# An attention, expert and mixer kernel on one core: batch 0's value products in float32, and every stage-1 score by one float32 product

## Chip, core and metric

One core of a Trainium2 chip runs the whole program. The metric is the device time of one execution in microseconds; lower is better. TensorE (PE in the rows, with its weight loads as PEld), VectorE (DVE), ScalarE (ACT), GpSimd (POOL) and the queue engine SyncE (SP) each run their own list of instructions in order and wait for one another through semaphores.

## What is computed

Three stages follow one another, for 4 batches of 576 positions. Stage 1 is attention with 8 heads of 64 and a decay by the cumulated logarithm of f. Stage 2 is attention by 4 experts over the 512 columns that stage 1 gives, mixed by a gate that keeps the best two. Stage 3 is a mixer over positions and a two-layer network of width 2048.

```python
scores = scale * q @ k.T + (cum[:, None] - cum[None, :])     # stage 1, 32 heads, causal
x = softmax(scores) @ v
...
y = sum over e of w[e] * (softmax(scale * (x wq[e]) (x wk[e]).T) @ (x wv[e])) @ wo[e]   # stage 2, 16 heads
...
u = y + (y.T @ U @ V).T                                       # stage 3
out = u + relu(u @ w_ch1) @ w_ch2
```

## The kernel before

**Order.** The kernel is written as many small generators, one for each piece of work. A planner (class `Plan`) resumes them by estimated times, a penalty `PEN` times a priority from the table `PR`, and for some pieces a choice of engine (`Any`, with the handicaps in `BIAS`). What it writes down is a fixed order on each engine. `HEADS` is the order in which score products are made: the 8 heads of batch 0, then `NEXT[b]` heads of the next batch, then the 4 expert heads of batch b, then the rest of the next batch.

**Precision.** Most products must be better than float16. An operand is split into a float16 high part and a float16 rest (`split`, or `parts` for exponentials), and a product is made by three float16 products (`TERMS`).

**Scores.** The first `WHOLE` = 10 heads of stage 1 have one float32 product per block of rows (`YW` tiles, 68 rows of operands: 64 of the head and 4 that carry the decay). The other 22 heads have two rounded-float32 products: one with `X`, which holds high parts and rests, and one with `Y`. For these, `load_heads` issues three loads from GpSimd's queue (`Y`, and `X` twice) and one from SyncE's (`R`), and `lows` makes two subtractions on GpSimd.

**Softmax.** `softmax` (five blocks of rows, 64 to 576 columns) finds the maxima on VectorE and the exponentials on ScalarE into `sc`. From there two ways lead to the value product. A pair of heads within `TURN` is turned on TensorE (`turn_head`): 15 transposes into PSUM, five copies to float16 on ScalarE and five rests on VectorE, both into `pt`. Other pairs are split first (`parts` into the tiles `P`, high part on ScalarE or VectorE, rest on VectorE or GpSimd) and turned by DMA transposes from SyncE's queue. `TURN` holds all of batch 0 (8 heads and 4 experts) and the first pair of batch 1.

**Values.** `values(b)` loads v into `vr` and splits it into `V1`; `values_gates` splits the experts' values into `V2`. `pair_pv` makes the value product of a head, 15 blocks times three terms, 65 columns each (the 65th sums the exponentials), and `pv_out` divides.

**Weights and the filler.** `prep` turns float64 weights into float32 with ScalarE, VectorE and GpSimd; `fold` multiplies wo into w_ch1 (`wfr`); `wf_scaled` and `w2_scaled` split `wfr` and `w2x` in two. `mix(b)` ends with the split of z(b) on ScalarE and VectorE. From then on `hidden` (`hid<-z,wfr`) and `outputs` (`acc<-w2x,g`) have work for batch b. It fills TensorE between the products of later heads.

Of the kernel before, what the change touches and what calls it, by code (L numbers as in the profile page):

```python
# [25 lines left out]
BIAS = {'act': 100.0, 'dve': 1000.0, 'pool': 0.0}  # L26
# [5 lines left out]
XHB = 1  # L32
PBUFS = (1, 1, 1)
VGAT = (2, 2)
EARLY = 11
WHOLE = 10
QUEUE = ('act', 'act', 'sp', 'act')
ACTDMA = 100
PEN = 13.823999999999998
# [5 lines left out]
PR = {'load': 2.75, 'low0': -1.5, 'low': 6.0, 'zeros': -2.0, 'scores': 3.25, 'soft0': 1, 'soft2_0': 1.0, 'soft': 5.5, 'soft2_': 7.0, 'pv0': -1.0, 'pv': 1.75, 'pvout0': 2.0, 'pvout': 4.75, 'project0': 3.75, 'project': 2.25, 'vg0': 0.75, 'vg': 4.75, 'out0': 1.0, 'out': 3.0, 'values0': 1.0, 'values': -1.0, 'wall': 5.25, 'prep': 6.5, 'f64': -1.25, 'f64_2': 3.25, 'fold': 2.25, 'wf': 1.75, 'w2': 3.75, 'mix': 0.25, 'relu': 0.0, 'store': 2.75, 'hidden': 6.25, 'outputs': 8.25}  # L45
TERMS = ((0, 0), (0, 1), (1, 0))

TURN = {(1, 0): 4, (2, 0): 2, (1, 1): 1, (1, 2): 0}

NEXT = (2, 0, 0, 0)  # L50
# [193 lines left out]
def attn_moe_mixer(ctx: ExitStack, tc: tile.TileContext, qk, v, f, wall, wot, wo, w1, w2, u3, v3, out):  # L244
# [161 lines left out]
    V2 = [const.tile([128, KB, 4, 65], F16, name=f"V2{i}") for i in range(2)]  # L406
    V1 = [[const.tile([128, KB, 2, 65], F16, name=f"V1{i}{n}") for n in range(VB[1])] for i in range(2)]
# [16 lines left out]
    r_X, r_Y = ring(XYB[0], "X"), ring(XYB[1], "Y", [68, 2, 576], F32R)  # L424

    YW = [r_Y.make([128, 2, 576], F32, f"YW{i}") for i in range(min(XYB[1], WHOLE))]
    r_Y.first = [YW[(i - WHOLE) % XYB[1]] for i in range(WHOLE)]
    r_R = ring(1, "R", [128, 576], F32)
# [6 lines left out]
    r_vr = ring(VB[0], "vr", [128, KB, 128], F32)  # L435
# [14 lines left out]
    l_v2 = lock("v2")  # L450

# [22 lines left out]
    def load_heads():  # L474
        for i, key in enumerate(HEADS):
            kind, b, h = key
            if i == 2:
                yield ev("rows of first")
            if i < WHOLE:
                Y = yield r_Y  # L480
                HG[key] = (Y,)
                HY[key] = Y
                yield QUEUE[1]
                n = count(2, "loaded", key)
                n.done(dma(HG[key][0][0:64], qk[b, h].rearrange("t d s -> d t s"), queue(1)).t)
                spawn(rows(n, b * H + h, Y), 0)
            elif kind == 1:
                X = yield r_X.of([128, 2, 576], F32R, "X")
                Y = yield r_Y
                HG[key], HY[key] = (X, Y), Y  # L490
                src = qk[b, h].rearrange("t d s -> d t s")
                n = count(4, "loaded", key)
                yield "pool"
                high = [dma(Y[0:64], src, nc.gpsimd)]
                yield "pool"
                high.append(dma(X[64:128], src, nc.gpsimd))
                R = yield r_R
                yield "sp"
                got = dma(R, qk[b, h].rearrange("t d s -> (t d) s"))
                yield "pool"  # L500
                n.done(dma(X[0:64, 1, :], qk[b, h, 1], nc.gpsimd).t)
                spawn(lows(n, X, Y, R, high, got), PR['low0' if b == 0 else 'low'])
                spawn(rows(n, b * H + h, Y), 0)
# [18 lines left out]
    def rows(n, i, Y):  # L522
        yield ev("aug", i // H)
        if id(Y) in map(id, YW):
            yield ev("rows", id(Y))
        yield QUEUE[0]
        a = aug[i]
        n.done(dma((Y if id(Y) in map(id, YW) else Y.bitcast(F32))[64:68], bass.AP(tensor=a.tensor, offset=a.offset, ap=[[S, 4], [2 * S, 2], [1, S]]),
                   queue(0)).t)
        if i == 0:  # L530
            ev("rows of first").done()
# [4 lines left out]
    def lows(n, X, Y, R, high, got):  # L536
        yield got
        for i, H_ in enumerate((Y, X)):
            yield high[i]
            yield "pool"  # L540
            o = slice(64 * i, 64 * i + 64)
            pool("tensor_tensor", X[o, i, :], in0=R[o], in1=H_[o, i, :].bitcast(F32), op=ALU.subtract)
            n.done()
        r_R.free(R)


    def scores():
        yield ev("mask")
        for key in HEADS:
            yield ev("loaded", key)  # L550
            whole, early = key in HEADS[:WHOLE], key in HEADS[:EARLY]

            ops = [(x[:, 0], x.rearrange("d t s -> d (t s)")) for x in HG[key]]
            for blk in range(KB):
# [4 lines left out]
                for c0, c1 in ([(0, n)] if n <= 512 else [(0, 288), (288, 576)]):  # L559
                    w = max(c1 - c0, 256) if key[0] == 1 and not whole else c1 - c0  # L560
# [11 lines left out]
            if key[0] == 1:  # L572
                r_Y.free(HY.pop(key))
# [68 lines left out]
    def turn_head(key):  # L642
# [5 lines left out]
        for c, blks, k0, k1 in ((0, (0, 1), 0, 5), (3, (2,), 0, 5), (6, (3,), 0, 5), (10, (4,), 0, 4), (14, (4,), 4, 5)):  # L648
# [15 lines left out]
            def out_(r=r, bank=bank, flat=flat, c=c, i=i):  # L664
                hi, lo = (pt[:, 15 * t + c:15 * t + c + i, :].rearrange("k c q -> k (c q)") for t in range(2))
# [30 lines left out]
    def pair_pv(kind, b, p):  # L696
# [7 lines left out]
        on_pe = p < TURN.get((kind, b), 0)  # L704
# [4 lines left out]
        for j in range(2):  # L709
# [17 lines left out]
            for blk in range(KB):  # L727
# [11 lines left out]
        if kind == 1:  # L739
            for i in range(2):  # L740
                r_vp[i].free(vs[i])
        elif p == 1:
            l_v2.free(l_v2.held)

    def pv_out(kind, b, p, j, bank, pv):

        h = 2 * p + j
        if kind == 1:
# [5 lines left out]
        if kind == 1:  # L754
            ts(rr, pv[:, :, 64], EPS, ALU.add, RV[b][p // 2], ALU.mult)
        else:
            ts(rr, pv[:, :, 64], EPS, ALU.add)
# [10 lines left out]
        tt(xn, pv[:, :, 0:64], rr[:, :, None].to_broadcast([128, KB, 64]), ALU.mult)  # L768
# [28 lines left out]

    def values(b):

        es, ss, last = [], [], []  # L800
        for half in range(2):
            mx = col(f"mxv{b}{half}", 2)
            vrs = []
            for i in range(2):
                vr = yield r_vr
# [4 lines left out]
                got = dma(vr, v[b][:, :, hp * 128:(hp + 1) * 128], queue(3))  # L810
                vrs.append((vr, got))
            for i, (vr, got) in enumerate(vrs):
                yield got
                junk = yield r_xn.of([128, KB, 128], F16, "junk")
# [6 lines left out]
            if half == 1:  # L821
# [4 lines left out]
                RV[b] = [times(f"rv{b}{i}", s, SV[b][1]) for i, s in enumerate(ss)]  # L826
                ev("sv", b).done()
            for i, (vr, got) in enumerate(vrs):
                hp = 2 * half + i
                hi = yield r_vp[0]  # L830
                lo = yield r_vp[1]
                VP[b, hp] = (hi, lo)
                x = vr.rearrange("p k (h d) -> p k h d", h=2)
                yield from split(hi[:, :, :, 0:64], lo[:, :, :, 0:64], x, ss[half])
                r_vr.free(vr)
# [42 lines left out]
    def values_gates(b):  # L878
# [13 lines left out]
        def out_(tb, nr, pp):  # L892
            x = pp[:nr, :256].rearrange("p (h d) -> p h d", h=4)
            yield from split(V2[0][:nr, tb, :, 0:64], V2[1][:nr, tb, :, 0:64], x, float(2.0 ** -PROJ_EXP))
# [466 lines left out]
    def zero_rows():  # L1361
        for y in YW:
# [6 lines left out]
    def zeros():  # L1369
# [5 lines left out]
        for hl in range(2):  # L1375
# [9 lines left out]
            nc.gpsimd.memset(V2[hl][64:128, 4, :, :], 0.0)  # L1385
            plan.cost += 250
            for t in [V2[hl], *V1[hl]]:
                yield "pool"
                nc.gpsimd.memset(t[:, :, :, 64:65], 1.0 - hl)
                plan.cost += 120  # L1390
# [15 lines left out]
    spawn(zeros(), PR['zeros'])  # L1406
    spawn(scores(), PR['scores'])
# [64 lines left out]
```

## Time and profile before

| | |
|---|---|
| median of 3 runs | 783.21 us (783.13 to 785.93) |
| profiled execution: its time, its span | 780.9 us, 779.2 us |
| TensorE busy, weight loads busy | 672.5 us (86%), 468.7 us (60%) |
| VectorE, ScalarE, GpSimd busy | 488.5 us (63%), 426.4 us (55%), 302.0 us (39%) |
| mean granted TensorE clock | 0.938 |

The four splits of z(b) start at 230.1, 380.9, 535.3 and 666.6 us in the trace. Busy time is the sum of an engine's instructions; TensorE's overlap one another, so its busy time is an upper reading. The span runs from the first instruction to the last, and 1.7 us of the execution lie around it. [...]

### The profile page before, as it was taken

The page shows a single profiled execution, that of the slowest core. Times are in us where ns is not written, and L with a number is a line of the kernel's source. Part 1 is how long each engine was busy: PE and PEld are TensorE (multiplying, and loading weights), DVE is VectorE, ACT ScalarE, POOL GpSimd, SP SyncE. Part 2 cuts the span into 40 slices and gives each one's busy share as a digit, 9 for nine tenths or more (in the row PEclk, how much of TensorE's full clock was granted, in tenths as well). Part 3 has the DMA queues.
Part 4 walks back from the last instruction along what each step waited for, and adds up shares of the span by engine and source line. Part 5 has one row for each costly group of instructions (what it writes and reads, how often), then busy time and mean ns, then how long its engine had stood idle before and what let it go on. Part 6 is the DMA issues. An engine that isn't in the chain of part 4 may idle for free. (4 is left out here: it accounts for less than half of the span.)

```text
span 779.2 us, 15886 instructions
## 1 busy us (share of the span) xinstructions
PE 672.5 (86%) x5810; PEld 468.7 (60%) x5810; DVE 488.5 (63%) x1573; ACT 426.4 (55%) x894; POOL 302.0 (39%) x364
## 2 busy tenths in 40 slices
PE   3777899986476999999699898996999999899996
PEld 2456678665453667666466575664677656555653
DVE  5798876778989854776866367657672763311111
ACT  3676775787686953656666346557562752212121
POOL 4133143236885630477675115666750241000000
PEclk9998999996855999999899999997999999999998
DMA  8534344677995855999997649999973775000000
GB/s 223 145 84 133 77 133 144 173 191 198 165 231 115 166 99 118 150 206 203 235 197 158 128 99 184 190 187 234 188 147 46 165 110 73 28 1 27 1 28 28
DMA packets 203234, 105.40 MB, mean 135 GB/s; under 512 B 164756, under 2 KB 184212, under 8 KB 203124
## 3 DMA queue, kind: packets, MB, share of 16 engines
q1 hardware_dynamic: 182740, 79.37, 51.2%
q0 software_dynamic: 8096, 16.22, 10.7%
q10 hardware_dynamic: 12320, 8.78, 4.1%
q8 instruction: 46, 0.75, 0.4%
q14 instruction: 32, 0.26, 0.1%
HBM read 51.90 MB, written 5.16 MB: 73 GB/s over the span
## 5 line engine op out<-in xcount | busy, mean ns | idle before, releaser
L262 PE MATMUL acc<-w2x,g 128*128 128x512 f16 x768 | 180.2, 380 | 0.5 <-ACT g L267 0.4
L285 POOL TENSOR_TENSOR P<-sc,P 64x64 f16<-64x64 f32 (+4 forms) x127 | 98.2, 779 | 139.4 <-ACT P L267 108.8
L262 PEld LDWEIGHTS <-g 128*128 128x128 f16 x864 | 82.4, 98 | 85.0 <-issue 0.7
L267 ACT ACTIVATE sc<-sc,nm 128x576 f32<-128x576 f32 (+4 forms) x185 | 100.3, 555 | 45.4 <-DVE nm L273 39.1
L262 PE MATMUL hid<-z,wfr 128*128 128x256 f16 x864 | 116.3, 284 | 8.7 <-DVE z L273 3.9
L273 DVE SCALAR_TENSOR_TENSOR g<-hid,g 128x512 f16<-128x512 f32 x72 | 49.6, 689 | 117.6 <-ACT g L267 117.6
L262 PEld LDWEIGHTS <-wfr 128*128 128x128 f16 x864 | 84.5, 101 | 33.7 <-issue 8.8
L267 ACT ACTIVATE g<-hid 128x512 f16<-128x512 f32 x72 | 42.5, 590 | 101.4 <-PE acc L262 72.4
L267 ACT ACTIVATE P<-sc 128x448 f16<-128x448 f32 (+4 forms) x167 | 71.7, 458 | 23.3 <-DMA pt<-P 21.5
L262 PE MATMUL mm<-V,pt 128*128 128x65 f16 x2058 | 75.6, 198 | 4.7 <-DMA pt<-P 3.4
L262 PEld LDWEIGHTS <-pt 128*128 128x128 f16 x2058 | 71.1, 101 | 8.0 <-DMA pt<-P 4.1
L262 PE MATMUL sp<-X 128*128 128x256 f32 (+1 forms) x132 | 53.7, 416 | 23.7 <-DVE nm L273 13.9
L273 DVE TENSOR_TENSOR P<-sc,P 128x576 f16<-128x576 f32 (+4 forms) x43 | 36.4, 847 | 30.8 <-ACT P L267 30.4
L273 DVE CUSTOM_DVE_ANT_0 sc<-sp,mask 128x448 f32<-128x448 f32 (+4 forms) x110 | 46.3, 425 | 9.5 <-POOL P L285 3.9
L285 POOL TENSOR_TENSOR xh<-xn,xh 128x320 f16<-128x320 f32 x29 | 26.3, 908 | 66.9 <-ACT xh L267 56.8
L262 PEld LDWEIGHTS sp<-X 128*128 128x128 f32 x132 | 28.3, 214 | 38.0 <-DVE nm L273 22.2
L262 PE MATMUL mm<-xt,wall 128*128 128x288 f16 x384 | 49.5, 286 | 0.0
L285 POOL TENSOR_TENSOR x<-x,sg 128x512 f32<-128x512 f32 (+2 forms) x18 | 23.1, 1286 | 65.8 <-DVE x L273 52.2
L262 PE MATMUL sp<-Y 68*128 68x256 f32 (+1 forms) x132 | 43.5, 336 | 0.0
L262 PEld LDWEIGHTS <-wall 128*128 128x128 f16 x384 | 37.5, 98 | 9.0
L273 DVE CUSTOM_DVE_ANT_0 sc<-sp,mask,cols 128x320 f32<-128x320 f32 (+4 forms) x75 | 35.8, 486 | 7.2 <-POOL P L285 3.8
L285 POOL TENSOR_TENSOR X<-R,Y 64x576 fp32r<-64x576 f32 x22 | 32.3, 1468 | 15.4 <-DMA R<-in_qk 15.2
(153 smaller groups left out, 1223.5 us busy)
## 6 DMA issues: line engine op xcount, KB each, us to landing
wd<-in_w SPq DMA_DIRECT2D x32, 512.0 KB
Y<-in_qk POOLq DMA_DIRECT2D x22, 288.0 KB, 4.8
R<-in_qk SPq DMA_DIRECT2D x22, 288.0 KB
X<-in_qk POOLq DMA_DIRECT2D x22, 288.0 KB, 6.0
vr<-in_v ACTq DMA_DIRECT2D x16, 320.0 KB
out_dram<-o SPq DMA_DIRECT2D x18, 256.0 KB
Xh<-stg SPq DMA_DIRECT2D x16, 216.0 KB
X<-in_qk POOLq DMA_DIRECT2D x22, 144.0 KB, 4.8
```

The source lines that it names most:

```text
L262: nc.tensor.matmul(out_, lhsT=lhsT, rhs=rhs, start=start, stop=stop, **kw)
L267: nc.scalar.activation(out_, in_, fn, **kw)
L273: getattr(nc.vector, op)(**kw)
L285: getattr(nc.gpsimd, op)(out=out_, **kw)
```

## The change

Scores: the split forms `X`, `R` and `lows` are gone. All 32 heads of stage 1 load one `Y` tile (a ring of three) from ScalarE's queue and have one float32 product per block. Value products of batch 0: `turn_head` copies the turned exponentials once, as float32; v stays in `vr` as loaded, the experts' values go to `V2F` as float32; `pair_pv` makes one float32 product per block where three float16 ones stood. The float16 tiles of values share their space with these float32 tiles and are prepared by `halves_v1` and `halves_v2` when batch 0 is done with them. The pair of batch 1 leaves `TURN`. The planner's tables change as well.

```diff
-BIAS = {'act': 100.0, 'dve': 1000.0, 'pool': 0.0}
+BIAS = {'act': 400.0, 'dve': 1800.0, 'pool': 0.0}
-EARLY = 11
-WHOLE = 10
+EARLY = 14
-TURN = {(1, 0): 4, (2, 0): 2, (1, 1): 1, (1, 2): 0}
+TURN = {(1, 0): 4, (2, 0): 2}
-NEXT = (2, 0, 0, 0)
+NEXT = (2, 0, 4, 0)
...
-            if i < WHOLE:
-                Y = yield r_Y
...
-            elif kind == 1:
-                X = yield r_X.of([128, 2, 576], F32R, "X")
...
-                spawn(lows(n, X, Y, R, high, got), PR['low0' if b == 0 else 'low'])
+            if kind == 1:
+                HY[key] = yield r_Y
+                HG[key] = (HY[key],)
                 yield QUEUE[1]
                 n = count(2, "loaded", key)
+                n.done(dma(HY[key][0:64], qk[b, h].rearrange("t d s -> d t s"), queue(1)).t)
+                spawn(rows(n, b * H + h, HY[key]), 0)
...
+                if as_is(*key[:2]):
+                    to = pt.rearrange("k c q -> k (c q)").bitcast(F32)[:, 128 * c:128 * (c + i)]
+                    if (yield Any(act=110 + 0.833 * 128 * i, dve=110 + 1.04 * 128 * i)) == "act":
+                        copy_scaled(to, flat[:, :128 * i])
+                    else:
+                        dve("tensor_copy", out=to, in_=flat[:, :128 * i])
...
-            for blk in range(KB):
+            for blk in range(KB if whole else 0):
+                yield "pe"
+                for kb in range(blk + 1):
+                    g = 128 * ((0, 1, 3, 6, 10)[blk] + kb)
+                    mm(pv[:, blk, :], pt.rearrange("k c q -> k (c q)").bitcast(F32)[:, g:g + 128],
+                       vs[:, kb, 65 * j:65 * j + 65] if kind == 1 else V2F[:, kb, 2 * p + j, :], blk + kb == 0, kb == blk,
+                       rate=1.7, skip_group_check=True)
+            for blk in range(0 if whole else KB):
...
+    def as_is(kind, b):
+
+        return b == 0 and TURN.get((kind, b), 0) == (4, 2)[kind - 1]
...
+                if as_is(1, b):
+                    VP[b, hp] = vr
+                    ev("vp", b, hp).done()
+                    continue
...
+            if as_is(2, b):
+                yield "act"
+                copy_scaled(V2F[:nr, tb, :, 0:64], x, float(2.0 ** -PROJ_EXP))
```

On TensorE, at the first value products of batch 0 (before; `V_78` and `V_80` are a high part and a rest of v, each product with its own weight load of `pt`):

```order
L658 MATMUL mm<-identr,sc_100 128x128 x4
L262 MATMUL sp<-YW_96 128x320
L262 LDWEIGHTS pt
L262 MATMUL mm<-V_78,pt 128x65
L262 LDWEIGHTS pt
L262 MATMUL mm<-V_78,pt 128x65
L262 LDWEIGHTS pt
L262 MATMUL mm<-V_80,pt 128x65
```

The same place after the change (`vr_79` is v as loaded; a float32 product carries its weight loads in itself):

```order
L632 MATMUL hid<-identr,sc_98 128x128 x3
L261 MATMUL mm<-vr_79,pt 128x65 x10
L261 MATMUL mm<-identr,cols 128x128
L632 MATMUL hid<-identr,sc_99 128x128 x4
L261 MATMUL mm<-vr_79,pt 128x65 x5
L261 MATMUL acc<-Y_94 128x288 x2
```

A head's 45 float16 products became 15 float32 products; they are cut in two only where the planner put transposes between them.

On VectorE, one head of batch 0 before (`ISA sp` and `ISA acc` are the passes that add the mask and find the maxima, `ISA nm` reads them out, `pt` rows are the rests of turned exponentials):

```order
L273 SCALAR_TENSOR_TENSOR pt<-hid,pt 128x512
L273 ISA sp,nm<-sp,mask 128x448
L273 ISA nm 128x1
L273 SCALAR_TENSOR_TENSOR pt<-mm,pt 128x128
L273 SCALAR_TENSOR_TENSOR pt<-mm,pt 128x384
L273 ISA acc,nm<-acc,mask 128x288
L273 ISA nm 128x1
L273 SCALAR_TENSOR_TENSOR pt<-hid,pt 128x384
L273 ISA acc,nm<-acc,mask,nm 128x288
```

And after:

```order
L272 ISA sp,nm<-sp,mask 128x448
L272 ISA nm 128x1
L272 ISA acc,nm<-acc,mask 128x288
L272 ISA nm 128x1
L272 ISA sp,nm<-sp,mask 64x64
L272 ISA nm 64x1
L272 ISA acc,nm<-acc,mask,nm 128x288
```

The rests are gone from VectorE; no copy of turned exponentials stands there in their place, all 60 stand on ScalarE.

On GpSimd, while heads of batch 1 are loaded (before):

```order
L293 DMA Y<-in_qk 64x2x576
L285 TENSOR_TENSOR wfr<-wfr 128x512
L293 DMA X<-in_qk 64x2x576
L285 TENSOR_TENSOR P_75<-sc_100,P_75 128x448
L293 DMA X<-in_qk 64x576
L285 TENSOR_TENSOR P_75<-sc_101,P_75 128x576
L285 TENSOR_TENSOR X<-R,Y 64x576
```

These loads are on ScalarE's queue after the change:

```order
L266 ACTIVATE y<-xn 128x5x64
L266 ACTIVATE sg,cols<-w2x 128x512
L292 DMA Y_94<-in_qk 64x2x576
L292 DMA Y_94<-aug 4x2x576
L266 ACTIVATE w2x<-wd 128x512
```

GpSimd loses 66 loads and 44 subtractions; ScalarE gains 22 loads of heads. GpSimd gets 50 more rests of exponentials (`P`), and the rests of 13 of the 16 pieces of `w2x`, in two instructions each, which VectorE had.

## Rows read from the trace of the kernel before

**Rows 1.** Stretches: length, busy PE PEld DVE ACT POOL (instructions), clock, DMA share, GB/s.

```profile
20.00:230.10 210.10, 164.75 (x1534) 131.11 (x1533) 176.87 (x526) 153.31 (x335) 84.83 (x78) 0.89 0.60 151
230.10:250.30 20.20, 11.14 (x72) 6.53 (x72) 19.76 (x47) 13.94 (x23) 13.39 (x14) 0.64 0.74 144
250.30:380.90 130.60, 124.93 (x1160) 86.01 (x1159) 88.60 (x319) 82.24 (x174) 67.80 (x82) 0.99 0.90 162
380.90:535.30 154.40, 137.09 (x1281) 95.36 (x1281) 97.52 (x364) 85.25 (x185) 78.65 (x96) 0.96 0.95 172
535.30:666.60 131.30, 124.57 (x1139) 84.56 (x1139) 75.15 (x261) 64.10 (x137) 48.33 (x61) 0.96 0.69 125
666.60:779.20 112.60, 103.36 (x612) 60.66 (x612) 18.92 (x32) 20.26 (x33) 0.00 (x0) 0.97 0.05 19
```

**Rows 2.** TensorE's waits, 20 to 230 us (total, times, longest).

```profile
PE hid L658 <- DVE pt L273: 10.9, 8, 3.2
```

**Rows 3.** Products hid of z: durations min/median/max, first and last start.

```profile
L262 PE MATMUL hid<-z,wfr x864: 269/273/437, 250.3 to 761.1; 128*128 128x256 f16 x173
```

**Rows 4.** TensorE's waits, 230 to 779 us.

```profile
PE sp L262 <- DVE nm L273: 16.4, 21, 2.3
PE sp L262 <- POOL X L285: 6.1, 3, 2.5
```

**Rows 5.** Busy time of pt alone: PE, PEld, DVE, ACT, then clock and DMA.

```profile
20.00:230.10 210.10, 26.25 (x672) 25.55 (x672) 37.68 (x70) 33.01 (x70) 0.89 0.60 151
```

**Rows 6.** Groups by shape: busy us, mean ns, idle before.

```profile
L273 DVE SCALAR_TENSOR_TENSOR V<-vr,cols,V 128x640 f16<-128x640 f32 x16 | 16.8, 1051 | 0.9 <-ACT V L267 0.9
L267 ACT ACTIVATE P<-sc 128x448 f16<-128x448 f32 (+4 forms) x167 | 71.7, 458 | 23.3 <-DMA pt<-P 21.5
L285 POOL TENSOR_SCALAR wfr<-wfr,cols 128x512 f32<-128x512 f32 x2 | 3.1, 1559 | 0.0
L285 POOL TENSOR_TENSOR wfr<-wfr 128x512 f16<-128x512 f32 x2 | 2.3, 1170 | 0.1
```

**Rows 7.** Timeline, float16 value products (start, duration, engine, line).

```profile
124.94 1.55 PE L262 MATMUL mm<-V,pt 128*128 128x65 f16 x45
```

**Rows 8.** All float16 value products of `pt`: durations min/median/max.

```profile
L262 PE MATMUL mm<-V,pt x2058: 191/193/262, 40.3 to 651.3; 128*128 128x65 f16 x188
```

**Rows 9.** Timeline, 28.5 to 29.6 us: float32 products and their weight loads.

```profile
28.54 0.52 PE L658 MATMUL hid<-identr,sc 128*128 128x128 f32 x3
28.79 0.53 PEld L262 LDWEIGHTS sp<-YW 128*128 128x128 f32 x4
28.90 0.71 PE L262 MATMUL sp<-YW 128*128 128x64 f32 x4
...
29.45 0.38 PE L262 MATMUL mm<-identr,cols 128*128 128x128 f32 x2
```

**Rows 10.** Instructions of YW: durations min/median/max, first and last start.

```profile
L262 PEld LDWEIGHTS sp<-YW x80: 186/192/338, 14.9 to 111.5; 128*128 128x128 f32 x80
...
L262 PE MATMUL acc<-YW x40: 406/406/688, 19.3 to 113.0; 128*128 128x288 f32 x40
L293 ACTq DMA_DIRECT2D YW<-in_qk x10: 602/629/662, 1.5 to 80.3; - x10
```

**Rows 11.** Timeline, TensorE: score products of a head in X and Y.

```profile
352.94 0.28 PE L262 MATMUL sp<-X 128*128 128x256 f32 x1
...
353.59 0.47 PE L262 MATMUL sp<-X 128*128 128x448 f32 x1
...
354.11 0.83 PE L262 MATMUL hid<-z,wfr 128*128 128x256 f16 x6
354.70 0.38 PE L262 MATMUL sp<-X 128*128 128x288 f32 x1
...
355.06 0.83 PE L262 MATMUL hid<-z,wfr 128*128 128x256 f16 x6
```

**Rows 12.** Timeline, TensorE, 27.3 to 28.6 us: float32 products of 288 columns.

```profile
27.39 1.14 PE L262 MATMUL acc<-YW 128*128 128x288 f32 x4
```

More of the change, by code (lines that the diff above doesn't have):

```diff
@@ L44 @@
 PROJ_EXP = 15
[L45 removed]
+PR = {'load': 2.0, 'low0': 0.25, 'low': 1.25, 'zeros': 3.5, 'scores': 1.75, 'soft0': 0.5, 'soft2_0': -2.0, 'soft': 2.25, 'soft2_': 6.5, 'pv0': 1.25, 'pv': 5, 'pvout0': 0.25, 'pvout': 0.75, 'project0': 3.75, 'project': 4.0, 'vg0': -1.5, 'vg': 4.0, 'out0': -0.75, 'out': 3.0, 'values0': 0, 'values': 0.0, 'wall': 5.25, 'prep': 5.0, 'f64': 1.0, 'f64_2': 1.25, 'fold': -0.25, 'wf': 0.5, 'w2': 7.25, 'mix': -1.0, 'relu': 2.5, 'store': -1.0, 'hidden': 1.75, 'outputs': 6.25}
 TERMS = ((0, 0), (0, 1), (1, 0))
[L48 to L50 removed]
+TURN = {(1, 0): 4, (2, 0): 2}
+NEXT = (2, 0, 4, 0)
 HEADS = [(1, 0, h) for h in range(8)]
@@ L423, in attn_moe_mixer @@
     r_acc = ring(1, "acc", [128, 2, 512], F32, ps)
[L424 to L428, printed above, removed]
+    Y = [const.tile([128, 2, 576], F32, name=f"Y{i}") for i in range(XYB[1])]
+    r_X, r_Y = ring(XYB[0], "X"), lock("Y", *Y)
     SC = [const.tile([128, 128 * (i + 1)], F32, name=f"sc{i}") for i in range(KB)]
@@ L559, in scores @@
                 for c0, c1 in ([(0, n)] if n <= 512 else [(0, 288), (288, 576)]):
-                    w = max(c1 - c0, 256) if key[0] == 1 and not whole else c1 - c0
+                    w = c1 - c0
                     sp = both[:, len(st)] if both is not None else (yield r_sp)
@@ L738, in pair_pv @@
             r_pt0.free(pt0)
-        if kind == 1:
+        if kind == 1 and whole:
+            l_vr.free(vs)
+        elif kind == 1:
             for i in range(2):
                 r_vp[i].free(vs[i])
+        elif p == 1 and whole:
+            spawn(halves_v2(), 0)
         elif p == 1:
@@ L795, in natural, with halves_v1, halves_v2 @@
         return YN[b].bitcast(F16).rearrange("q (p t c d) -> q p t c d", p=2, t=2, c=KB)
+    def as_is(kind, b):
+        return b == 0 and TURN.get((kind, b), 0) == (4, 2)[kind - 1]
+    def halves_v1():
+        yield v1_free
+        for hl in range(2):
+            for t in V1[hl]:
+                yield "pool"
+                nc.gpsimd.memset(t[:, :, :, 64:65], 1.0 - hl)
+                plan.cost += 120
+        ev("v1").done()
+    def halves_v2():
+        for hl in range(2):
+            yield "pool"
+            nc.gpsimd.memset(V2[hl][64:128, 4, :, :], 0.0)
+            plan.cost += 250
+            yield "pool"
+            nc.gpsimd.memset(V2[hl][:, :, :, 64:65], 1.0 - hl)
+            plan.cost += 120
+        l_v2.free(l_v2.held)
     def values(b):
@@ L825, in values @@
                 SV[b] = scales(f"v{b}", e, 14)
-                RV[b] = [times(f"rv{b}{i}", s, SV[b][1]) for i, s in enumerate(ss)]
+                RV[b] = [SV[b][1] if as_is(1, b) else times(f"rv{b}{i}", s, SV[b][1]) for i, s in enumerate(ss)]
                 ev("sv", b).done()
@@ L1361, in zero_rows @@
     def zero_rows():
-        for y in YW:
+        for y in Y:
             yield "pool"
@@ L1383, in zeros @@
                     plan.cost += 130
-            yield "pool"
[L1385 to L1390, printed above, removed]
+        yield "pool"
+        nc.gpsimd.memset(V2F[64:128, 4, :, :], 0.0)
+        nc.gpsimd.memset(V2F[:, :, :, 64:65], 1.0)
+        plan.cost += 370
+        for t in [*VR, *V1F]:
+            yield "pool"
+            nc.gpsimd.memset(t[:, :, 0:130:129], 1.0)
+            plan.cost += 120
         ev("zeros").done()
@@ L1406, in attn_moe_mixer @@
     spawn(zeros(), PR['zeros'])
+    spawn(halves_v1(), PR['zeros'])
     spawn(scores(), PR['scores'])
```

82 lines of the change are left out of this document (34 added, 48 removed).

## The prediction

> **What bounds the kernel now.** I read the table of stretches first [rows 1], with its borders at the points where `mix` splits z(b), because from z(0) on TensorE has the filler (`hid`, `acc`) and before it has none. The stretch from 20 to 230.1 us, the front, holds batch 0's attention, its experts and the preparation of the weights. The reader is to see that no engine is full there, but that VectorE comes nearest: 176.9 of 210.1 us (84%), against 164.8 for TensorE at a clock of 0.89, 153.3 for ScalarE and 84.8 for GpSimd. TensorE's waits in the front [rows 2] say the same: what it waited for longest is the rest of turned exponentials on VectorE, which holds a PSUM bank, 10.9 us in 8 waits. Between 230.1 and 250.3 VectorE is busy 19.8 of 20.2 us with weight splits, and the first `hid` stands only at its end [rows 3]. From 250.3 on TensorE is busy 92 to 96% of each stretch but one (89%), and is the bound.
>
> For a sum I need TensorE's useful time. As a rough measure I multiply its busy time with the granted clock. The front holds 164.8 x 0.89 = 147 us. Behind z(0) the loss, length less that product, is 20.2 - 11.1 x 0.64 = 13 us, then 7, 23, 12 and 12 us in the four later stretches [rows 1]: 67 us of 549. Part of it is waits of score products for VectorE (16.4 us, by the bank that the maxima pass frees) and for GpSimd's X (6.1 us) [rows 4].
>
> So the time is three terms: when z(0) comes, what TensorE has to do behind it, and what is lost behind it.
>
> **VectorE, ScalarE and GpSimd in the front.** All 70 rests of `pt` go, 37.7 us of VectorE, and all lie in the front [rows 5]. The four value splits of batch 0 go too: 4 x 1.05 = 4.2 us on VectorE [rows 6], and as many instructions on ScalarE, which I leave out. VectorE falls from 176.9 to 135 us. The copies fall from 70 to 60, and each writes as many elements as before; at 33.0 / 70 = 0.47 us [rows 5] ScalarE loses 4.7 us. The two heads of batch 1 that leave `TURN` add ten pieces of `P` at 0.46 [rows 6], +4.6. ScalarE stays at 153. GpSimd was far from full and is no bound in the front.
>
> **TensorE in the front.** A head's 45 float16 products took 1.55 us [rows 7]; the last one alone lasts 0.19 [rows 8], so 0.031 us pass from one to the next. The float32 product of 65 columns isn't in the trace. The nearest is that of 64 columns [rows 9]: each float32 product is two rows, each with its own weight load, and the merged row of four products holds two of 64 columns and two of 192. Their four loads last 0.53 us together and one lasts 0.19 [rows 10], so they start (0.53 - 0.19) / 3 = 0.113 us apart. If the loads set the pace, a product costs 2 x 0.112 = 0.224 us. If they hide behind the products, the time goes by columns: the four rows up to the next start span 29.45 - 28.90 = 0.55 us for 512 columns, 0.14 for a product of two times 64. I take 0.224, since 15 such products follow one another with new weights each time and nothing wide stands between them; the low end is 0.14. With 8 + 4 heads of 15 products, 180 x 0.224 = 40.3 us take the place of 540 x 0.031 = 16.7: **+23.6 us** (low end +8).
>
> [...]
>
> Thirty transposes of the two heads go, three in 0.52 us, tail included [rows 9], so 0.17 each at most; I take 0.13: -4. Two of the 22 changed heads have their scores ahead of z(0): +1.6 by the price below. TensorE's 147 become 168 us.
>
> So VectorE's 177 as the largest load of the front gives way to TensorE's 168, with ScalarE at 153. The largest load filled 84% of the front; TensorE filled (124.9 x 0.99) / 130.6 = 95% of the stretch behind 250.3, where it had filler. Midway, 168 / 0.90 = 187 us, puts z(0) at 207: **-23 us**. The ends are 168 / 0.84 = 200 (-10) and, with the cheap float32 product, 153 / 0.90 = 170 for either engine (-40).
>
> **Scores behind z(0).** A head with X and Y costs, from start to start [rows 11]: a 256 pair and the 320 pair 0.65 (352.94 to 353.59), the other 256 pair 0.3 at most, 448 0.52, 288 twice 0.36: 2.2 us, and about 2.0 without the small waits in it. In float32 it costs 0.55 for 64 and 192 columns [rows 9] and, for 288, (1.14 - 0.41) / 3 = 0.243 from row to row [rows 10, 12], four times, 0.97. By columns, 320 and 448 add 2 x 768 / 288 x 0.243 = 1.30: 2.8 us. The other 20 heads pay 0.8 each: **+16 us** (0.6 to 1.1: +12 to +22), and this lies where TensorE is the bound. ScalarE's queue takes over 22 loads; their issue is some 0.63 us each [rows 10], 14 us spread over an engine busy 82 of 131 us in the fullest stretch behind 250.3. They hide; if not, a score would wait for its exponentials by the same amount. SyncE and GpSimd lose 88 issues and 44 subtractions.
>
> **What is lost behind z(0).** The splits of `wfr` stand in the new order well ahead of z(0) on ScalarE; before, three of eight stood ahead of it. So `hid` can start with z(0): I take back 10 of the 13 us of that stretch. The waits for X (6.1) go, and part of the 16.4 for VectorE, but the tails at the end of each batch stay. I take **-14 us**. Ends: -25 (all these waits go) and +10, where GpSimd is late: 13 rests of `w2x` now cost 1.56 + 1.17 us there [rows 6], 35 us, ahead of the first outputs.
>
> **Sum.** 780.9 (the profiled execution) - 23 + 16 - 14 = 760; the median of the runs shown lies 2.3 above that execution, so 762 for the median. A difference of 0.5%, 4 us, is what this measurement tells from none.
>
> **Rivals.**
> *The front falls further.* The weight loads hide behind the products; TensorE and ScalarE have 153 us each in the front: 780.9 - 40 + 16 - 14 = 743. For it: the span of 0.55 us is explained by columns alone. Against: the spacing of 0.113.
> *The front doesn't move.* ScalarE sets it, in its order: 153 before and after. Then 0 + 16 - 14 = +2: 783. For it: ScalarE loses nothing. Against: it was busy 73% there and VectorE 84%.
> [...]
> *GpSimd holds the outputs up* by `w2x`: 760 + 24 = 784, from the +10 end.
> That the change doesn't do what it says is excluded by the order: no rest of `pt` in batch 0 and no X is left.
>
> **How the numbers follow.** Forecast 0.47 (its own range 750 to 775), front falls further 0.20, front doesn't move 0.13, low clock 0.12, GpSimd 0.08. Faster by over 0.5%: the first two and a little of the third, 0.70. Within: most of the third and half of the fourth, 0.13. Slower: 0.17. The range reaches from 738 (the second rival) to 788; above lies most of the low-clock case, below a front that shrinks with hidden loads and all waits gone.
>
> **What would show it.** Right: the first split of z at 200 to 214 us; float32 products of 65 columns 0.22 us apart; `hid` within 10 us of that split; about 2.8 us of TensorE for a score head; 90 to 100 us less VectorE in all. Wrong: z(0) later than 225, a clock under 0.8 in the front, TensorE waiting for `w2x` on GpSimd, or score products waiting for a `Y` load on ScalarE's queue.

## The result, and the profile after

The change makes the kernel slower: 792.10 us against 783.17 us, medians of 20 runs each on one chip; the ratio is 1.0131, 95% interval 1.0108 to 1.0154. The ratio leaves out three of the 40 runs, in which the whole execution ran slower. The forecast was 762, its range ended at 788.

The profiled execution took 795.17 us. Its page, busy times and the granted clock in 40 slices:

```profile
PE 698.4 (88%) x5600; PEld 486.7 (61%) x5600; DVE 411.9 (52%) x1435; ACT 423.1 (53%) x890; POOL 298.1 (38%) x354
...
PEclk9999999985979999999999999999999999999999
```

VectorE lost 76.6 us (488.5 before), TensorE gained 26. The stretches again have their borders at the splits of z(b), but the front is cut in two where `project` begins (115.4 us before, 135.5 after); busy times of PE, PEld, DVE, ACT, POOL, then clock, DMA share and GB/s:

```profile
20.00:135.50 115.50, 104.21 (x745) 90.96 (x746) 78.46 (x244) 85.50 (x181) 43.28 (x47) 0.99 0.55 138
135.50:233.40 97.90, 76.09 (x539) 60.41 (x538) 69.96 (x207) 68.09 (x154) 50.46 (x47) 0.85 0.61 153
233.40:384.60 151.20, 128.97 (x1188) 86.47 (x1187) 86.78 (x345) 94.15 (x195) 90.36 (x97) 0.98 0.72 128
384.60:554.50 169.90, 157.18 (x1501) 106.47 (x1500) 99.97 (x416) 105.79 (x230) 78.86 (x97) 1.00 0.80 146
554.50:653.00 98.50, 96.03 (x852) 63.77 (x851) 44.20 (x163) 41.46 (x89) 26.67 (x33) 1.00 0.49 97
653.00:793.30 140.30, 131.86 (x775) 76.03 (x773) 23.08 (x38) 24.43 (x39) 0.00 (x0) 0.98 0.04 16
```

The same two halves of the front before:

```profile
20.00:115.40 95.40, 76.99 (x723) 59.63 (x723) 82.89 (x266) 70.34 (x151) 24.51 (x21) 0.95 0.43 115
115.40:230.10 114.70, 87.77 (x813) 71.49 (x811) 93.98 (x262) 82.97 (x185) 60.32 (x57) 0.84 0.74 181
```

Three things are to be seen. The first half grew by 20.1 us. There TensorE is now busy 104.2 of 115.5 us at a clock of 0.99, where VectorE (82.9 of 95.4) had been the fullest; VectorE's own work fell by only 4.4 us there, since other work moved in. The second half shrank by 16.8, and there VectorE lost 24.0; z(0) comes at 233.4, 3.3 later than before. Behind z(0) lie 559.9 us instead of 549.1: the three stages up to z(3) are 16.9 shorter in all than before, the last stretch 27.7 longer, because filler was left over for it (775 instructions of TensorE instead of 612).

TensorE's value products on its timeline (start, duration), from the first half and from the second:

```profile
63.26 1.45 PE L261 MATMUL mm<-vr,pt 128*128 128x65 f32 x12
...
178.55 12.95 PE L261 MATMUL mm<-V,pt 128*128 128x65 f32 x60
```

The twelve rows of 1.45 us start 0.112 us apart, and that is the median of the 300 such rows that ran at a granted clock of 1.00; a product has two rows, so it costs 0.224. The 60 rows at 178.55 start 0.21 apart: the granted clock was 0.50 from the first of them to the last (0.51 in the wider stretch that the last section shows). This is called the low clock below.

The filler: `hid` follows z(0) at once (it began 20 us behind it before [rows 3]), `acc` with w2x does not. Durations min/median/max, first and last start:

```profile
L261 PE MATMUL hid<-z,wfr x864: 269/273/417, 237.6 to 775.6; 128*128 128x256 f16 x173
```

```profile
L261 PE MATMUL acc<-w2x,g x768: 376/379/381, 267.5 to 786.5; 128*128 128x512 f16 x192
```

Before, that `acc` began at 253.7 us. The rests of w2x on GpSimd end only at 324:

```profile
L284 POOL TENSOR_SCALAR w2x<-w2x,cols x14: 326/1562/1564, 133.0 to 320.0; 128x512 f32<-128x512 f32 x13, 128x16 f32<-128x16 f32 x1
L284 POOL TENSOR_TENSOR w2x<-w2x x13: 1143/1157/1162, 246.4 to 322.8; 128x512 f16<-128x512 f32 x13
```

TensorE's waits from 230 us on, in answer to [rows 4]:

```profile
PE sp L261 <- DVE nm L272: 16.0, 27, 1.7
PE hid L261 <- DVE g L272: 8.0, 9, 2.0
PE acc L261 <- POOL w2x L284: 2.7, 2, 1.8
```

### The profile page after: what moved, and what is told of

It reads as the page before. It is cut to its first block, busy times and chain, and to the rows that moved or that the text cites. A ratio compares the mean times of both kernels' runs of the same rounds, so it can differ in the third digit from the quotient of the medians.

```text
span 793.3 us, 15199 instructions
## 1 busy us (share of the span) xinstructions
PE 698.4 (88%) x5600; PEld 486.7 (61%) x5600; DVE 411.9 (52%) x1435; ACT 423.1 (53%) x890; POOL 298.1 (38%) x354
## 4 chain that ended last, share of the span: by engine, by line
PE 37%; DMA 7%; DVE 7%; ACT 3%; POOL 2%; issue 2%; ACTq 1%; DVEq 0%; SPq 0%; POOLq 0%
PE acc L261 16%; PE hid L261 9%; PE mm L261 9%; DMA pt<-P 6%; PE sp L261 3%; DVE sc L272 3%; POOL P L284 2%; ACT sc L266 1%; ACT P L266 1%; DVE g L272 1%; DVE rr L272 1%; DVE cols L272 1%; ACTq L292 1%; DMA Xh<-stg 1%; DVE nm L272 1%
## 5 line engine op out<-in xcount | busy, mean ns | idle before, releaser
L284 POOL TENSOR_TENSOR P<-sc,P 128x448 f16<-128x448 f32 (+4 forms) x177 | 140.7, 809 | 168.7 <-ACT P L266 140.1
L261 PE MATMUL sp<-Y 128*128 128x320 f32 (+4 forms) x344 | 105.2, 428 | 28.7 <-DVE nm L272 18.0
L266 ACT ACTIVATE P<-sc 128x192 f16<-128x192 f32 (+4 forms) x180 | 77.4, 461 | 34.6 <-DMA pt<-P 19.5
L261 PEld LDWEIGHTS sp<-Y 128*128 128x128 f32 x344 | 58.2, 198 | 57.4 <-DVE nm L272 35.5
L261 PE MATMUL mm<-V,pt 128*128 128x65 f16 (+1 forms) x1752 | 87.8, 209 | 1.1 <-DMA pt<-P 1.1
L272 DVE CUSTOM_DVE_ANT_0 sc<-sp,mask 128x320 f32<-128x320 f32 (+4 forms) x110 | 46.7, 428 | 19.9 <-POOL P L284 15.7
L272 DVE CUSTOM_DVE_ANT_0 sc<-sp,mask,cols 64x64 f32<-64x64 f32 (+4 forms) x60 | 29.1, 488 | 16.6 <-PE sp L261 9.2
L261 PE MATMUL hid<-x,wtr 128*128 128x128 f32 x256 | 33.2, 284 | 4.4 <-POOL x L284 4.4
L261 PE MATMUL sp<-Xh 128*128 128x64 f16 (+4 forms) x176 | 30.1, 285 | 5.9 <-DVE nm L272 3.7
L261 PEld LDWEIGHTS hid<-x,wtr 128*128 128x128 f32 x256 | 31.0, 197 | 7.2 <-POOL x L284 5.9
```

What stands on the lines that cost most here:

```text
L261: nc.tensor.matmul(out_, lhsT=lhsT, rhs=rhs, start=start, stop=stop, **kw)
L266: nc.scalar.activation(out_, in_, fn, **kw)
L272: getattr(nc.vector, op)(**kw)
L284: getattr(nc.gpsimd, op)(out=out_, **kw)
```

## The experiments

All 17 runs, and the two kernels. The ratio is to the kernel before, run on the same chip; project, z(0) and what lies behind z(0) are us of the one profiled execution. That execution can lie several us off its kernel's median (795.2 against 792.1 in the changed kernel, 787.3 against 782.5 in changed_w2_on_vector), so a few us in these columns show nothing by themselves. Where an edit is made to the kernel's text, the planner lays out a new order; such a run prices the edit together with its order. Only products_twice, products_bf16, scores_bf16 and w2_rests_left_out keep the changed kernel's order.

| run | ratio, 95% interval | project | z(0) | behind |
|---|---|---|---|---|
| before | 1 | 115.4 | 230.1 | 549.1 |
| changed | 1.0131 (1.0108 to 1.0154) | 135.5 | 233.4 | 559.9 |
| values_only | 1.0184 (1.0129 to 1.0240) | 133.8 | 243.0 | 556.0 |
| scores_only | 1.0326 (1.0284 to 1.0367) | 114.6 | 227.2 | 577.0 |
| both_old_tables | 1.0317 (1.0274 to 1.0360) | 134.1 | 233.5 | 572.1 |
| tables_only | 1.0486 (1.0444 to 1.0528) | 130.0 | 232.5 | 585.6 |
| no_f32_values | 1.0378 (1.0338 to 1.0418) | 129.6 | 232.1 | 578.4 |
| f32_heads_only | 1.0385 (1.0328 to 1.0443) | 136.1 | 229.3 | 578.0 |
| f32_experts_only | 1.0067 (1.0021 to 1.0113) | 129.8 | 232.5 | 548.4 |
| scores_only_y_by_sync | 1.0060 (1.0030 to 1.0090) | 113.8 | 221.2 | 560.1 |
| both_old_y_by_sync | 1.0094 (1.0060 to 1.0128) | 133.7 | 233.2 | 551.4 |
| changed_y_by_sync | 1.0271 (1.0217 to 1.0325) | 135.1 | 238.7 | 565.8 |
| scores_y_sync_f32_experts | 0.9988 (0.9955 to 1.0021) | 115.5 | 232.3 | 546.0 |
| changed_w2_on_vector | 1.0032 (0.9999 to 1.0066) | 135.6 | 229.2 | 556.3 |
| changed_w2_vector_f32_experts | 1.0104 (1.0068 to 1.0141) | 125.6 | 237.9 | 557.7 |
| products_twice | 1.0581 (1.0502 to 1.0659) | 161.5 | 263.0 | 559.2 |
| products_bf16 | 0.9883 (0.9828 to 0.9939) | 126.0 | 216.2 | 556.7 |
| scores_bf16 | 1.0140 (1.0071 to 1.0210) | 136.6 | 239.0 | 555.2 |
| w2_rests_left_out | 1.0100 (1.0064 to 1.0136) | 135.1 | 225.4 | 556.0 |

**The parts apart.** values_only is the kernel before with `V2F`, `VR`, `as_is` and what calls them:

```diff
-            for blk in range(KB):
+            for blk in range(KB if whole else 0):
...
+                    mm(pv[:, blk, :], pt.rearrange("k c q -> k (c q)").bitcast(F32)[:, g:g + 128],
...
```

> The kernel before with the value part of the change alone (batch 0's exponentials and values stay float32; score products and every table as before). Theory A, TensorE takes VectorE's place in the first half of the front (until project starts): the 24 us of added TensorE work lie where TensorE is then full, so z(0) stays at 226 to 238 us (230.1 before) and the time at 779 to 792. Theory B, the step of the prediction (the front is one pool, filled to 0.90 by its largest load): z(0) near 207 and a time of 757 to 765. Theory C, the new tables ate the gain by moving the fold into the first half: with the old tables z(0) comes at 210 to 222 and the time is 763 to 775.

scores_only is the kernel before with one `Y` per head and no `X`:

```diff
-            whole, early = key in HEADS[:WHOLE], key in HEADS[:EARLY]
+            whole, early = key[0] == 1, key in HEADS[:EARLY]
...
```

> The kernel before with the score part alone (one float32 product for each score of stage 1, Y by ScalarE's queue, no X; values and every table as before). Theory A, the work lies where TensorE is the bound: 20 heads at 0.8 us, +16, less at most the 6 us of waits for X, so +8 to +18: 791 to 801, all of it behind z(0), and z(0) within 4 us of 230. Theory B (prediction): the price is paid back by the waits for X and VectorE that go: +2, 781 to 788. Theory C, the tables are what costs behind z(0): within 5 us of before.

no_f32_values is the changed kernel without the float32 values. both_old_tables has both parts, with the tables of before:

```diff
-BIAS = {'act': 400.0, 'dve': 1800.0, 'pool': 0.0}
+BIAS = {'act': 100.0, 'dve': 1000.0, 'pool': 0.0}
...
```

> The changed kernel with the tables of before (BIAS, XHB, VGAT, EARLY, PEN, PR, NEXT and the turned pair of batch 1). Theory A: the sum of the two parts alone, so within 5 us of the changed kernel, 786 to 798. Theory C, the tables cost the gain (fold ahead of project, rests of w2x on GpSimd, first outputs late): 765 to 778, with z(0) at 222 or less and the first acc within 22 us of z(0).

> The changed kernel with batch 0's values and exponentials as float16 pairs again (the changed tables and scores stay). Theory A, TensorE and VectorE only change places in the front: z(0) at 226 to 240 us and a time within 6 us of the changed kernel, 785 to 798. Theory D, the float32 value products are the loss (24 us of TensorE and its low clock in a stretch where it is full): z(0) at 215 to 224 and a time of 774 to 783. Theory B (prediction): without them VectorE is the largest load again, z(0) comes 20 us later, 805 to 820.

The front behaved as theory A has it, and worse: with values in float32 `project` came 18 to 20 us later in the old order, and z(0) not one microsecond earlier in any of the three pairs (230.1 to 243.0, 227.2 to 233.5, 232.1 to 233.4). In both_old_tables none of the 360 float32 rows ran at the low clock (0.93 over the second half of its front), so the low clock is not what lost the gain there. Theory C fell: the new tables are not what lost the gain, since both parts with the old ones are slower than the kernel before too (and still are further down, with the queue out of the way: 1.0094). But no theory had foreseen that the parts do not add up, and all four kernels took longer than theory A allows: values_only 799.2 (792 at most), scores_only 807.5 (801), both_old_tables 807.2 (798), no_f32_values 811.8 (798). The last of these times lies in theory B's range, but not by its mechanism: z(0) is in place at 232.1, and the loss lies behind it. scores_only cost 28 us behind z(0).

**Where scores_only loses.** ScalarE's timeline (ACTq: what its queue issues):

```profile
312.50 0.66 ACTq L292 DMA_DIRECT2D Y<-in_qk  x1
313.20 0.73 ACTq L292 DMA_DIRECT2D Y<-aug  x1
313.97 0.62 ACTq L292 DMA_DIRECT2D Y<-in_qk  x1
314.63 1.24 ACTq L292 DMA_DIRECT2D Y<-aug  x1
315.92 0.61 ACTq L292 DMA_DIRECT2D Y<-in_qk  x1
323.48 0.25 ACTq L292 DMA_DIRECT2D Y<-aug  x1
323.77 0.38 ACT L266 ACTIVATE V<-mm 64x256 f16<-64x256 f32 x1 [10.89 <-DMA Y<-aug]
```

Three heads' loads stand in a row; the sixth is issued 7.0 us behind the fifth's end, and a copy of V that wants no Y waits behind it, 10.89 us in all. VectorE waits 7.1 us for that copy and TensorE's `hid` 8.0 for VectorE's rest of g. This happens again at 461 us, for 5.8: a copy of V behind the sixth load waits 9.12 us there.

What held the load is named by the chain of work that ended last in this stretch:

```profile
312.31 11.15 DMA pt<-P
323.46 0.02 issue
323.48 0.25 ACTq L292
```

By it the load waits for a transpose that SyncE's queue issued at 312.31, and goes out 0.02 us after that one has landed. The wait at 461 us ends with such a transpose too (466.71; the load goes out at 466.74), and the changed kernel's wait of 4.5 us at 498.6 with the landing of an `Xh` load of SyncE's queue (503.12). So ScalarE stood behind a transfer of another queue.

```diff
-                yield QUEUE[1]
+                yield QUEUE[1] if i < 10 else "sp"
...
```

> The kernel with the score part alone, but the loads of Y for all heads behind the first ten on SyncE's queue. In scores_only ScalarE's queue stood twice at the sixth of six Y loads in a row, 7.0 and 5.8 us, and hid waited 25.6 us for g. Theory Q, these loads hold ScalarE up and with it the filler: hid's waits for g fall under 12 us and the time falls by 8 to 18 us, to 789 to 799. Theory A, the loss is the work of the scores on TensorE alone: within 5 us of scores_only, 803 to 812. Rival: on SyncE's queue the loads stand behind transposes and score products wait for Y: 810 to 830.

It came to 784.9 us, a ratio of 1.0060 instead of 1.0326: some 21 us, theory Q, and more than it asked. `hid` waited 10.7 us for g instead of 25.6, which are 15 of them; the rest may lie in the new order. So with the old tables most of the score part's price hung on this queue. Three kernels more with those loads on SyncE:

> The changed kernel with the loads of Y for all heads behind the first ten on SyncE's queue. Theory Q, these loads on ScalarE's queue cost the changed kernel as they cost scores_only (22 us there): 768 to 780. Theory A, in the changed kernel's order ScalarE's queue stood only 4.5 us at one of them (498.6 us): the gain is 2 to 8 us, 784 to 790. Rival: SyncE's queue, which carries the transposes of P and the loads of wd, holds the scores up: 795 or more.

> Both parts of the change with the tables of before, and the loads of Y behind the first ten heads on SyncE's queue: against scores_only_y_by_sync (784.9 us, z(0) at 221.2) this prices the float32 values with ScalarE's queue out of the way. Theory A, the values move the limit of the first half from VectorE to TensorE: project 18 to 21 us later (132 to 135), z(0) 5 to 13 us later (226 to 234), time 788 to 800. Theory B (prediction): z(0) 20 us earlier, 762 to 770.

> scores_only_y_by_sync (tables of before) with float32 values for batch 0's four experts alone, whose products lie behind project where TensorE is not full. Theory A, there the 20 rests leave VectorE and the added 8 us of TensorE lie in a stretch with room: project as before (112 to 117), z(0) 0 to 6 us earlier (215 to 221), 777 to 785. [...]

In the changed kernel, whose queue stood 4.5 us only, SyncE's queue is the worse one: 799.7, the rival's time. Its mechanism doesn't show: score products waited for a Y load once there, 2.8 us (3.5 in the changed kernel). both_old_y_by_sync took 786.6, with `project` 19.9 and z(0) 12.0 us later than scores_only_y_by_sync: float32 values buy nothing in the front here either, theory A, and again no row of theirs ran at the low clock (0.93 over the second half of the front); the time is just under its range, since 8.7 us came back behind z(0). scores_y_sync_f32_experts can't be told from before: its time is theory A's, 778.8, but z(0) came at 232.3, later than its 215 to 221, with 44 of the experts' 120 rows at the low clock (0.84 over the second half of the front). No kernel here that keeps full precision was faster than the kernel before.

**Which value products matter.**

```diff
-        return b == 0 and TURN.get((kind, b), 0) == (4, 2)[kind - 1]
+        return kind in VALS and b == 0 and TURN.get((kind, b), 0) == (4, 2)[kind - 1]
...
```

f32_heads_only keeps float32 values for the eight heads alone, f32_experts_only for the four experts alone; the others' values are float16 pairs again. With the experts' products go, in the first, the 60 rows that took 12.95 us at the low clock; at 0.112 from row to row they would take an estimated 6.7.

> [...] Theory A: the first half stays as in the changed kernel (project at 130 to 140), the second half gives back the low clock, 13 us become 6 to 7, and VectorE gets 20 rests back: z(0) at 225 to 238, the time 785 to 798. Theory F, the low clock of that stretch is what the front lost: z(0) at 222 or less and 780 or less.

> The changed kernel with float32 values for batch 0's four experts alone; its eight heads' values are float16 pairs again. Theory A: TensorE loses 16 us ahead of project, VectorE gets 50 rests back there and becomes the limit again; project at 125 to 134, z(0) at 224 to 238. Theory D, the heads' float32 products lengthen the front and nothing takes their place: project at 115 to 122 and z(0) at 220 or less.

Without the eight heads' products TensorE was busy 17 us less ahead of `project`, but `project` came only 5.7 us earlier (129.8): VectorE was again the fullest engine (92.0 of 109.8 us), as theory A has it, and the clock there was 0.92 instead of 0.99. z(0) stayed. Theory A's z(0) and `project` held in both, its time for f32_heads_only did not: that kernel took 809.7 us, 18 of it more than the changed kernel behind z(0), for a reason that no run took apart.

**The price of the products in the changed order.** products_twice and products_bf16 leave the order of all engines as it is. The second reads only the upper halves of the float32 words, as bfloat16, and so leaves out the rest of each operand; what the other engines do is unchanged. At 0.031 us for such a product, the price of a float16 one before [rows 7], it spares TensorE an estimated 180 x (0.224 - 0.031) = 35 us, 23 of them ahead of `project`.

```diff
+                    nc.tensor.matmul(pv[:, blk, :], lhsT=x, rhs=y, start=False, stop=kb == blk, skip_group_check=True)
...
```

> The changed kernel in its own order, with each of batch 0's 180 float32 value products issued twice into the same sum (numerator and denominator double, so the values divide out). At full clock that adds 120 x 0.224 = 26.9 us of TensorE before project and 13.4 behind it. Theory A, TensorE is the bound of the first half of the front and its work there counts in full: project starts 22 to 32 us later (157 to 168) and z(0) 30 to 50 us later. Theory E, the first half is a chain through several engines in which TensorE only waits less: project by 150 and z(0) less than 20 us later. Theory B (the front as one pool that the largest load fills to 0.90): 208 / 0.90, so z(0) at 251, 18 us later, wherever the work lies.

The two halves of its front:

```profile
20.00:161.50 141.50, 130.59 (x984) 117.33 (x985) 78.69 (x244) 85.62 (x181) 42.53 (x45) 1.00 0.44 110
161.50:263.00 101.50, 81.81 (x660) 66.68 (x658) 68.74 (x207) 67.98 (x154) 50.94 (x48) 0.94 0.62 151
```

Of the 26.9 us added ahead of `project` 26.0 show. There TensorE is the bound for added work, product for product; theory B's 18 us fall. In the second half 3.6 show of 13.4, partly because the clock rose from 0.85 to 0.94; so z(0) came 29.6 us later, just short of theory A's 30.

```diff
-                    mm(pv[:, blk, :], pt.rearrange("k c q -> k (c q)").bitcast(F32)[:, g:g + 128],
+                    x = pt.rearrange("k c q -> k (c q)").bitcast(BF16)[:, 2 * g + 1:2 * g + 256:2]
...
```

> The changed kernel in its own order on all engines, but each of batch 0's 180 value products reads only the upper halves of the same float32 words, as bfloat16 (the lower halves are left out of the product). [...] Theory A, these products are the bound of the first half: project 12 to 23 us earlier (112 to 124) and z(0) 15 to 30 us earlier (203 to 218), the time 762 to 777; that is where the prediction had put z(0) with the products' cost counted in. Theory E, the first half hangs on a chain through other engines: project at 128 or later, z(0) at 226 or later, 785 or more.

```profile
20.00:126.00 106.00, 83.62 (x624) 68.27 (x625) 80.60 (x244) 84.21 (x181) 42.11 (x47) 1.00 0.57 150
126.00:216.20 90.20, 63.85 (x480) 46.96 (x479) 73.65 (x207) 68.36 (x153) 51.12 (x48) 0.82 0.68 167
```

z(0) and the time are theory A's; `project` missed its range by 2 us. Taking an estimated 23 us of TensorE's work away (its busy time fell by 20.6) gave 9.5 there: ScalarE (84.2), TensorE (83.6) and VectorE (80.6) are now at 76 to 79% of the 106 us. The 180 products kept TensorE busy 10.5 us here and 48.8 in the changed kernel. With products almost free, then, the change's relief brings z(0) from 230.1 to 216.2, 14 us; their price takes 17 back. Up to 8 of these 17 go with the 60 rows of the changed kernel that ran at the low clock (0.50): z(0) came at 225.4 in w2_rests_left_out, in which none did.

**Behind z(0), in the changed order.** scores_bf16:

```diff
+            if whole and HEADS.index(key) >= 10:
+                ops = [(x.bitcast(BF16)[:, 0, 1::2], x.bitcast(BF16).rearrange("d t s -> d (t s)")[:, 1::2]) for x in HG[key]]
```

The quarter in what was expected is the price of float16: in the changed kernel a `hid` row of 256 float16 columns took 0.109 us from row to row, 0.43 ns a column, and a float32 product of 288 columns two rows of 0.243, 1.69 ns a column. In products_bf16 a bfloat16 row of 65 columns lasted 195 and 206 ns (means), a float16 one 193.

> The changed kernel in its own order on all engines, but the score products of the stage-1 heads behind the first ten read only the upper halves of the same float32 words, as bfloat16 (the lower halves are left out of the product). A float32 head costs TensorE 2.8 us, 1600 columns at a quarter of that per column 0.7; 20 heads behind z(0) spare 20 x 2.1 = 42 us. If TensorE is the bound there and the work counts in full, the stretch behind z(0) falls from 559.9 to 518 to 528; if a third or more of it lies in gaps that other waits keep open, to 530 to 545; z(0) stays within 4 us of 233 (two of these heads stand ahead of it).

Both theories fell: 555.2 us lie behind z(0), 4.7 less than in the changed kernel. The two stretches with the scores, and TensorE's first wait from 230 us on:

```profile
239.00:388.10 149.10, 117.01 (x1139) 77.33 (x1139) 87.49 (x345) 94.25 (x195) 90.84 (x98) 0.94 0.69 129
388.10:556.20 168.10, 139.95 (x1430) 92.69 (x1429) 99.48 (x416) 105.99 (x230) 78.39 (x97) 0.97 0.80 148
```

```profile
PE sp L261 <- DVE nm L272: 40.5, 59, 2.4
```

TensorE is busy 29 us less there than in the changed kernel, and the stretches are 3.9 us shorter. The waits of score products for VectorE's maxima grew from 16.0 to 40.5 us, and the clock fell from 0.98 and 1.00 to 0.94 and 0.97. By the prediction's rough measure, busy time times clock, 38 us of work went: an estimated 9 of them went into the lower clock, some 24 into these waits, and 3.9 came out. So most of what the float32 products take stood where TensorE would have waited.

w2_rests_left_out:

```diff
+            if out_w2:
+                nc.gpsimd.memset(lo, 0.0)
...
```

> The changed kernel in its own order, with the 13 rests of w2x that stand on GpSimd left out: each of the two instructions, 1.56 and 1.16 us, gives way to one fill of the rest with zeros, so those rows of w2 keep only their first float16 part. GpSimd rival: the outputs start 5 to 15 us sooner behind the split of z(0) (34.1 us behind it in the changed kernel), the filler stands in the waits of the next stage instead of behind z(3), and the stretch behind z(0) falls from 559.9 to 548 to 556. Theory A, GpSimd's lateness costs only the 2.7 us that acc was seen to wait: 557 us or more.

Behind z(0) it took 556.0, 3.9 less, the least that the GpSimd rival asked, but the rival's mechanism did not show: `acc` still began 33.7 us behind z(0), where the order has it, and no longer waited for GpSimd. The ratio fell by 0.3%, and the two intervals overlap. Where the same rests go to VectorE, the planner lays the whole program out anew:

```diff
-        if src.space == PSUM or (yield Any(dve=170 + 1.04 * n, pool=2 * (180 + 1.93 * n))) == "dve":
+        if src.space == PSUM or on_dve or (yield Any(dve=170 + 1.04 * n, pool=2 * (180 + 1.93 * n))) == "dve":
...
```

> The changed kernel with all 16 rests of w2x on VectorE (before: 13 of them on GpSimd, the first outputs 30 us behind the split of z(0)). GpSimd rival: the outputs start within 20 us of that split, the filler fills the experts' waits earlier and the time falls by 5 to 15 us, 777 to 787. Theory A: GpSimd's lateness cost only the 2.7 us that acc waited for it, and the 16 rests load VectorE, on which score products wait: within 5 us of the changed kernel.

> The kernel before with the new tables alone (XHB stays 1, since two would not fit beside X; values and scores as before). GpSimd rival: most rests of w2x go to GpSimd, the first acc comes 28 to 40 us behind the split of z(0) and the time is 788 to 802. Theory A: the tables alone change little, 778 to 788, with z(0) at 226 to 234.

> The changed kernel with w2x's rests on VectorE and float32 values for the four experts alone: the two edits that gained by themselves (782.5 and 789.4 against 792.1). If they add up, 778 to 781, within 0.5% of before; if the relief of TensorE ahead of project is worth more once the outputs start in time, 770 to 776, faster than both kernels; if they are two ways to the same gain, 781 to 785.

changed_w2_on_vector gained as much as the GpSimd rival had it, to 782.5, but `acc` began 25.8 us behind z(0) and not within 20, and its order is another one; so this does not price GpSimd alone. tables_only was far worse than either theory: its scores wait 24.4 us for X on GpSimd, which the new tables load, and `acc` began only 24.8 us behind z(0). The two gains did not add up: a ratio of 1.0104, some 791 us, beyond all three cases. Part of it can be seen in one row, the second half of its front:

```profile
125.60:237.90 112.30, 95.14 (x639) 77.87 (x636) 74.61 (x213) 76.22 (x168) 61.94 (x55) 0.80 0.57 146
```

TensorE is busy 95.1 of 112.3 us, at a clock of 0.80; 90 of the experts' 120 float32 rows ran at the low clock, and z(0) came 8.7 us later than with VectorE's rests alone.

## Why the prediction was wrong, step by step

**The front: the step "168 / 0.90 = 187 us, puts z(0) at 207".** Its inputs were good. A product cost 0.224 us (0.112 from row to row); TensorE's load came to 104.2 x 0.99 + 76.1 x 0.85 = 168 us, ScalarE's to 153.6. VectorE's was 148.4, not 135, as it lost 76.6 us in all and not 90 to 100; it was not the fullest, so this did no harm. What failed is the 0.90: the load filled 168 of 213.4 us, 0.79. I had taken the front for one pool. It is two stages in a row. Up to `project` TensorE, with the value products in it, is busy 0.90 of the time (as I had guessed for the whole), and products added there lengthen it one for one. Behind it no engine is busy more than 0.78, TensorE's useful time is 64.7 of 97.9, and of the 13.4 us of products added there 3.6 show, at a risen clock; which of the waits between project, experts and mix set the length of that stage no run took apart. In the first stage TensorE at once took VectorE's place, and the stage grew by 20.1 us; the second gave 16.8 back. Predicted −23, measured +3.3: 26 of the 35 us between the sum (760) and the profiled 795.2. The experts' rows at the low clock explain 8 of the 26 at most: with none of them there (w2_rests_left_out) z(0) came at 225.4, which is −4.7 and still far from −23.

**The scores: "this lies where TensorE is the bound", +16.** The size was right: 448, 320, 288 and 192 columns took 0.376, 0.270, 0.243 and 0.162 us from row to row, 2.7 us a head. The place was misread. Taking 2.1 us a head away gave almost nothing back (scores_bf16). A busy TensorE was not a bound: with 29 us less to do there it waited 24.5 us more for VectorE's maxima (16.0 to 40.5). So at most a small part of the +16 is a price in this order, and most of the +10.8 measured behind z(0) has another source. That doesn't hold for every order: with the old tables and the queue out of the way (scores_only_y_by_sync) the score part still has 11.0 us more behind z(0), and z(0) 8.9 earlier, which no run took apart.

**The losses, −14.** `hid` at once behind z(0) and the end of the waits for X came true; the waits for VectorE did not shrink (16.4 to 16.0) and `hid` gained 5.6 us of waits for g (2.4 before). GpSimd's work on `w2x` is worth some 3.9 us in this order, by w2_rests_left_out. What it costs that the order puts the first `acc` 34 us behind z(0) was not priced alone, but over the runs the two do not go together: f32_experts_only has it 38.2 behind and 548.4 us behind z(0), scores_only 24.7 and 577.0. So some 7 of the 10.8 us stay open: the order leaves 27.7 us more for the stretch behind z(3), and which of its choices does that was not tried alone.

**ScalarE's queue, "they hide".** True in the changed order, where it stood 4.5 us; wrong in the old one, by about 21 us. It was also not the issue time that cost, but a load that had to wait for another queue's transfer.

**The rivals.** "The front doesn't move" has z(0) in place, but its 783 is 9 us short, and its reason is another one: ScalarE was said to set the front, and TensorE does in its first half. "Low clock", given 0.12, came true for 60 of 360 rows, at a granted clock of 0.50: 6 us in the rows (12.95 against 6.91), 8 at z(0). "GpSimd holds the outputs up" came true in its sign (`acc` late), not in its price.

## What to carry to other kernels

Cut a stretch where the fullest engine changes before dividing a load by a filling: two stages in a row give back only what the fullest engine of each gives. An engine that is busy 85% is a bound only if its work, taken away, shortens the stretch; an order kept fixed with one engine's work made cheaper or doubled tells that in one run. Before a load moves to a compute engine's queue, ask which other transfer it has to wait for, and what stands behind it in the queue until then.

## What the hardware showed beyond that

The same front, in one order, ended at 225.4, 233.4 and 239.0 us in three kernels (w2_rests_left_out, changed, scores_bf16), as 0, 60 and 120 of the experts' float32 rows ran at the low clock (over the second half of the front it was 0.93, 0.85 and 0.73); two of the last one's lighter score heads also stand there. One stretch of it, the changed kernel and then w2_rests_left_out:

```profile
178.00:195.00 17.00, 17.00 (x83) 15.66 (x82) 7.17 (x22) 6.49 (x15) 5.30 (x4) 0.51 0.43 128
```

```profile
178.00:195.00 17.00, 14.00 (x108) 11.25 (x107) 14.42 (x46) 12.31 (x28) 6.21 (x5) 1.00 0.38 115
```

In the 8 us ahead of it TensorE was busy 5.94 us in the one and 6.08 in the other, at a clock of 0.77 and 0.82; just ahead of the last transposes it had waited 1.64 and 1.07 us. In products_twice, with each of these products issued twice, no row ran at the low clock (0.94 over the second half of the front). So in one order the same 60 rows without a gap stood at a granted clock of 0.50 from the first to the last, or at 1.00: they cost 12.95 or 6.91 us. What decided it no run shows.
